# Loads reordered, and the folded matrix M built during batch 0's exps, in an attention and maxout MoE kernel

## The chip, the cores and the metric

The kernel runs on one core of one Trainium2 chip. The metric is device microseconds of one execution, as the median of the runs. The engines are TensorE (PE in the profile; PEld is its weight load), VectorE (DVE), ScalarE (ACT), GpSimd (POOL) and SyncE (SP). Each has an instruction queue of its own, which it works through in program order. Loads that convert float32 to bfloat16 on the way are issued by GpSimd; plain loads of q and k by SP.

## What is computed

Blockwise causal attention feeds a maxout MoE layer. Batch 8, heads 8, sequence 576, head size 64; d_model 512, d_ff 1024, 4608 tokens.

```python
scores = scale * np.matmul(q, k.transpose(0, 1, 3, 2))
mask = block_i >= block_j            # blocks of 64 positions
attn = softmax(np.where(mask, scores, -1e9))
x = np.matmul(attn, v).transpose(0, 2, 1, 3).reshape(B * S, H * D)
h1 = x @ w1
h2 = x @ w2
g = np.maximum(h1, h2)
out = g @ w_out
```

## The kernel before, in words

**Work units.** Two heads make a pair, four pairs a batch, two pairs a group (GPB is 2 groups per batch, NG 16 groups). Batch 0 (groups 0 and 1) is written out by hand in lines 578 to 682; groups 2 to 15 follow, group 2 partly in the hand-written part, groups 3 to 15 in the loop at line 684.

**Attention.** load_qk (L112) loads q and k of a group as float32, with SP or ACT as issuer; with gated=True GpSimd first writes one element of the new buffer (L119), so that the load is issued only when GpSimd has come to that point of its program. cast (L126) makes bfloat16, for the groups after the first two on GpSimd (L132). transposes (L346) turns q or k on TensorE (18 matmuls, L352) and copies the result out with two engines (L360), mostly half on VectorE and half on ScalarE. A burst (L402) or a tile (L432 to L457) puts scores of 512 columns in one of two PSUM buffers ps_s (L371), and one ScalarE exp (L395) writes them to aT; mask (L399) clears masked parts by memset. av (L463) multiplies by V (L479), and VectorE divides by the row sums (L485 and L486) into xp. x_out (L503) transposes xp on TensorE (L517, L519) and copies it into xT (L522, L523); from group 4 on a DMA transposes it instead. pad_keys (L377) copies the corner keys kz on GpSimd (L378). load_v (L134) loads one chunk of 128 rows of V through GpSimd (L136).

**MoE.** max(xw1, xw2) is computed as max(x(w1 - w2), 0) + xw2. d_sb = w1 - w2 comes from diff_w on VectorE (L162), in four quarters of 256 columns. The part xw2 is folded into the output: M = w2 w_out, so that out = max(xd, 0) w_out + xM. bT_unit (L223) transposes a quarter of w2 (8 matmuls, L227) into bT_sb (L229); m_unit (L234) makes one eighth of M (8 matmuls of 256 columns, L238). h_unit (L202) makes one of 8 column blocks of xd for a span of tokens (L215) and VectorE clips it to g (L220). y_unit (L252) sums 4 + 8 matmuls into 128 rows of the output (L257), which VectorE (first two spans) or ScalarE copies (L262) and SP stores. Spans 0 and 1 are the first 256 and the next 320 tokens, that is batch 0; later spans have 512 tokens. All MoE units, x_out, av and the transposes take their PSUM tiles from one pool of four buffers (tag "m"). warm_up (L338) runs matmuls on zeros that nothing reads (L341).

**Buffers for w2.** w2 has no tile of its own: it lies in parts of xT that later batches fill (L146 to L150).

**What sets the order.** plan (L285) writes a list of units with the tokens each needs and its cost per matmul (1 for 512 columns). fill(n) (L322) issues matmuls until n of cost are spent, each time from the first unit of the list whose tokens are there. In the list before, span 0's h units are mixed with the bT units, and the M units come behind span 1's h units. fill_of (L534) sets how much a group gets: the ready work less 6, spread over the groups left until the next batch. In groups 3 to 15 two ninths of it, at least 3, go ahead of each pair's av, an eighteenth, at least 3, into the middle of each av, and the rest to the end of the group. The loads are issued in program order of GpSimd's queue: V chunks 0 and 1, a quarter each of w1 and w2, V chunks 2 to 4, then the other quarters, and then the two halves of w_out (L168). Group 2's q is loaded by SP at the start, its k after V chunk 4.

Of the kernel before, what the change touches and what calls it, by code (L numbers as in the profile page):

```python
# [14 lines left out]
def kernel(  # L15
# [96 lines left out]
    def load_qk(g, queues, gated=False):  # L112
        b, u = divmod(g, GPB)
        for nm, src, queue in (("q", q, queues[0]), ("k", k, queues[1])):
            if queue is None:
                continue
            raws[nm, g] = t = raw.tile([P, 2, RPP * D], FP32, name=f"{nm}raw")
            if gated:
                nc.gpsimd.memset(t[:, 0, :1], 0.0)  # L119
            queue.dma_start(  # L120
                out=t[:],
                in_=src[b, 4 * u:4 * u + 4].rearrange(
                    "(s h) (p t) d -> (h p) s (t d)", h=2, t=RPP),
            )

    def cast(nm, g, parts):  # L126
        t = raws[nm, g].rearrange("p s (t d) -> p t s d", d=D)
        if (nm, g) not in qk_n:
            qk_n[nm, g] = qkn.tile([P, RPP, 2, D], BF16, name=f"{nm}n")
        n = qk_n[nm, g]  # L130
        for copy, j0, j1 in parts:
            copy(out=n[:, j0:j1], in_=t[:, j0:j1])  # L132
# [10 lines left out]
    wor = moe_w_out.rearrange("(c p) f -> p c f", p=P)  # L143

    WB = 256
    w1_raw, w2_sb = {}, []  # L146
    for j in range(d_ff // WB):
        row, n = (1, j) if j < 3 else (3, 0)
        t0 = 3 * S - 3 * BLK + n * NDM * WB
        w2_sb.append(xT[:, row, t0:t0 + NDM * WB].rearrange("p (c f) -> p c f", c=NDM))  # L150

    def load_w(j, which=(0, 1)):
        fs = slice(j * WB, (j + 1) * WB)
        if 0 in which:
            w1_raw[j] = wraw.tile([P, NDM, WB], FP32, name="w1raw")
            nc.gpsimd.dma_start(out=w1_raw[j][:], in_=w1r[:, :, fs])
        if 1 in which:
            nc.gpsimd.dma_start(out=w2_sb[j], in_=w2r[:, :, fs])

    def diff_w(j):  # L160
        fs = slice(j * WB, (j + 1) * WB)
        nc.vector.tensor_sub(d_sb[:, :, fs], w1_raw[j][:], w2_sb[j])  # L162

    WH = d_model // 2

    def load_wo(i):
        ds = slice(i * WH, (i + 1) * WH)
        nc.gpsimd.dma_start(out=wo_sb[:, :, ds], in_=wor[:, :, ds])  # L168
# [8 lines left out]
    nc.vector.memset(zeros[:], 0.0)  # L177
    nc.scalar.activation(out=warm[:], in_=warm[:], func=AF.Exp)
    load_qk(1, (SP, SP))
    load_qk(2, (SP, None))  # L180
    make_identity(nc, ident)
    for r in range(NV):
        nc.vector.memset(vv_r[r][:, :, :, D:D + 1], 1.0)
# [6 lines left out]
    cast("k", 0, ((act, 0, 5), (dve, 5, RPP)))  # L190
    for c in range(2):
        load_v(0, c)
    load_w(0, (0,))
    cast("q", 1, ((pool, 7, RPP),))
    cast("k", 1, ((pool, 0, 7),))
    load_w(0, (1,))


    done_tokens = [0]
# [23 lines left out]
    def bT_unit(j):  # L223
        pt = ps_m.tile([P, 2, NDM, P], BF16, name="ps_bT", tag="m")
        for i in range(2):
            for c in range(NDM):
                nc.tensor.transpose(pt[:, i, c, :], w2_sb[j][:, c, i * P:(i + 1) * P], ident[:])  # L227
                if i == 1 and c == NDM - 1:
                    nc.vector.tensor_copy(  # L229
                        out=bT_sb[:, 2 * j:2 * j + 2, :],  # L230
                        in_=pt.rearrange("p i c d -> p i (c d)"))
                yield

    def m_unit(i, c):  # L234
        ds = slice(i * WH, (i + 1) * WH)
        pt = ps_m.tile([P, WH], FP32, name="ps_M", tag="m")
        for f in range(NFF):
            nc.tensor.matmul(  # L238
                pt[:], bT_sb[:, f, c * P:(c + 1) * P], wo_sb[:, f, ds],
                start=(f == 0), stop=(f == NFF - 1),  # L240
            )
            if f == NFF - 1:
                nc.vector.tensor_copy(out=m_sb[:, c, ds], in_=pt[:])
            yield
# [40 lines left out]
    def plan():  # L285
        def h(i, f):
            t0, w = spans[i]
            units.append((h_unit(i, f), t0 + w, w / SPAN, NDM))

        def y(i, s, last=False):  # L290
            t0, w = spans[i]
            if last:
                units.append((y_last(i, s), t0 + w, 0.333, 3 * NY))
            else:
                units.append((y_unit(i, s), t0 + w, 1.0, NY))

        for i in range(NSPAN):
            for f in range(NFF):
                h(i, f)
                if i == 0 and f % 2:  # L300
                    units.append((bT_unit(f // 2), 0, 0.25, 2 * NDM))
                if i > 2 and f % 2 == 0 and f // 2 < tiles[i - 1]:
                    y(i - 1, f // 2)
            if i == 1:
                for n in range(2 * NDM):
                    units.append((m_unit(n // NDM, n % NDM), 0, 0.5, NFF))
                for j in range(2):
                    for s in range(tiles[j]):
                        y(j, s)
        n = tiles[-1]  # L310
        for s in range(n):
            y(NSPAN - 1, s, s == n - 1)
# [25 lines left out]
    def warm_up(n):  # L338
        pw = ps_m.tile([P, SPAN], FP32, name="ps_w", tag="m")
        for _ in range(n):  # L340
            nc.tensor.matmul(pw[:], zeros[:, :P], zeros[:], start=True, stop=True)  # L341
# [4 lines left out]
    def transposes(nm, g, copies):  # L346
        n = qk_n.pop((nm, g))
        pts = [ps_m.tile([P, RPP, NP], BF16, name=f"ps_{nm}T", tag="m") for _ in range(2)]
        for j in range(RPP):
            for i in range(2):  # L350
                r = slice(i * NP, (i + 1) * NP)
                nc.tensor.transpose(  # L352
                    pts[i][:, j, :], n[r, j].rearrange("p s d -> p (s d)"), ident[r, r],
                )

        def copy_out(which=(0, 1), part=(0, NP), copy=None):
            p0, p1 = part
            for i in which:
                t = (qT_r if nm == "q" else kT_r)[(2 * g + i) % NT]
                (copy or copies[i])(  # L360
                    out=t[:, p0 * RPP:p1 * RPP].rearrange("q (p j) -> q p j", j=RPP),
                    in_=pts[i][:, :, p0:p1].rearrange("q j p -> q p j"),
                )
        return copy_out
# [12 lines left out]
    def pad_keys(p):  # L377
        nc.gpsimd.tensor_copy(  # L378
            out=kz_r[p % NT].rearrange("p (a c) -> p a c", c=BLK)[:, 0:3:2],
            in_=kT_r[p % NT][:, S - 3 * BLK:].rearrange("p (a c) -> p a c", c=BLK)[:, 0:3:2],  # L380
        )
# [31 lines left out]
    def burst_q1(p):  # L413
        burst(p, ((0, QCUT, 320), (1, QCUT, 192)), 384)

    def burst_q2(p):
        burst(p, ((1, 448, P), (2, QCUT, 320), (4, 512, BLK)), 896)
# [4 lines left out]
    def masks_p(p, eng=None):  # L422
        for a in (0, 256):
            mask(p, a, eng)

    def masks_q(p, eng=None):
        for a in (1024, 1408):
            mask(p, a, eng)
# [3 lines left out]
    def tile_0(p):  # L432
        u = ps_s.tile([P, 2, 512], FP32, name="ps_s", tag="s")
        scores(p, u, 0, 0, 0, 512)
        return lambda: (exp(p, u, 512, 0), mask(p, 0))

    def tile_1(p):
        u = ps_s.tile([P, 2, 512], FP32, name="ps_s", tag="s")
        scores(p, u, 0, 0, 512, 64)
        scores(p, u, 64, 1, 128, 448)  # L440
        return lambda: (exp(p, u, 512, 512), mask(p, 576))
# [147 lines left out]
    burst_p(1)  # L589
    warm_up(2)  # L590
    masks_p(1)
    for c in range(2, NCH):
        load_v(0, c)
    load_qk(2, (None, SP), gated=True)
    load_w(1)
    cq = transposes("q", 1, (dve, dve))
    burst_q1(0)
    ck = transposes("k", 1, (dve, dve))
# [15 lines left out]
    masks_p(3, nc.vector)  # L614
    burst_q2(0)
    av(2, [0, 1])
    warm_up(2)
    x_out(0, 0, 2, (act, act))
    av(3, [0, 1])
    diff_w(0)  # L620
    burst_q1(1)
    warm_up(2)
    cast("q", 2, ((pool, 0, RPP),))
    masks_q(0)
    load_w(2)
    burst_q2(1)
    x_out(1, 0, 2)
    warm_up(2)
    burst_q3(1)
    masks_q(1)  # L630
    load_w(3)
    fill(4)
    burst_q1(2)
    transposes("q", 2, (dve, act))()
    burst_q2(2)
    av(0, [2, 3, 4])
    burst_q3(2)
    masks_q(2)
    cast("k", 2, ((pool, 0, RPP),))
    load_wo(0)  # L640
    load_wo(1)
    av(1, [2, 3, 4])
    burst_q1(3)
    burst_q2(3)
    av(2, [2, 3, 4])
    transposes("k", 2, (dve, act))()
    burst_q3(3)
    masks_q(3)
    pad_keys(4)
    pad_keys(5)  # L650
    for c in range(NCH):
        load_v(1, c)
    load_qk(3, (SP, SP), gated=True)
    x_out(0, 2, NCH)
    fill(2)
    diff_w(1)
    outs = tile_0(4), tile_1(4)
    av(3, [2, 3, 4])
    region(*outs)
    x_out(1, 2, NCH)  # L660
    fill(4)
    diff_w(2)
    fill(2)
    region(tile_2(4), tile_0(5))
    fill(4)
    diff_w(3)
    fill(2)
    region(tile_1(5), tile_2(5))
    fill(4)
    fill(2)  # L670
    cast("q", 3, ((pool, 0, RPP),))
    cast("k", 3, ((pool, 0, RPP),))
    n = fill_of(GPB)
# [86 lines left out]
```

## Time and profile before

| what | value |
|---|---|
| time, median of 3 runs (lowest, highest) | 260.99 us (260.83, 261.69) |
| the profiled execution: its time, its span | 260.99 us, 259.2 us |
| busy share of the span, PE / PEld / DVE / ACT / POOL | 94% / 54% / 53% / 55% / 42% |
| chain that ended last, share of the span | PE 85%, DMA 5%, POOL 3%, issue 2%, ACT 2% |
| weight and V loads by GpSimd's queue: packets, MB | 42272, 8.92 |
| q and k loads and stores by SP's queue: packets, MB | 28544, 31.27 |

The span runs from the first to the last instruction; the time also holds what lies around it, 1.8 us here. A row of a timeline gives the start, the length, the engine, the line of the kernel, the operation, out<-in and the number of instructions; in square brackets it gives the engine's idle time ahead of it and what ended that. A matmul's listed length holds its way through the array, so a matmul that follows another costs less than its length: the difference of two starts is its price. The times of loads below run from the issue to the landing of the last byte.

### The profile page before, as it was taken

The numbers are of one execution on the slowest core, as the hardware profiler recorded it, in microseconds if no ns is written. First come the engines' busy times: TensorE is split into PE (matmuls) and PEld (weight loads), VectorE is DVE, ScalarE is ACT, GpSimd is POOL, SyncE is SP. The second block draws the span as 40 slices with busy tenths as digits, with TensorE's granted clock in tenths as the row PEclk, the third lists the DMA queues.
The fourth block names the chain that finished last, engine by engine and source line by source line (L and its number), as shares of the span: only waits on it lengthen the run. The fifth ranks groups of instructions, "written<-read, shape, count | busy, mean of one in ns | idle before, by whom it ended". The sixth has DMA issues, their size and how long they took to land.

```text
span 259.2 us, 7161 instructions
## 1 busy us (share of the span) xinstructions
PE 244.8 (94%) x2949; PEld 139.4 (54%) x2983; DVE 137.6 (53%) x301; ACT 141.3 (55%) x198; POOL 109.8 (42%) x274
## 2 busy tenths in 40 slices
PE   8688799999999999999999999999999999999995
PEld 3346566856555545454646464646464655444444
DVE  4967996646584518451855185518550853453200
ACT  2798552766665766576657665776577431100111
POOL 2987914475638163816381638263823010000000
DMA  7999998789579995998599949984986122202122
GB/s 245 317 204 310 194 241 146 280 73 275 111 184 250 135 195 136 238 149 215 129 236 139 179 163 239 141 208 139 90 106 116 44 51 83 83 0 81 43 104 99
DMA packets 71265, 41.30 MB, mean 159 GB/s; under 512 B 53568, under 2 KB 58048, under 8 KB 71232
## 3 DMA queue, kind: packets, MB, share of 16 engines
q1 hardware_dynamic: 28544, 31.27, 41.4%
q0 software_dynamic: 42272, 8.92, 38.2%
q10 hardware_dynamic: 416, 0.66, 0.7%
q8 instruction: 23, 0.38, 0.6%
q14 instruction: 10, 0.08, 0.1%
HBM read 34.60 MB, written 9.44 MB: 170 GB/s over the span
## 4 chain that ended last, share of the span: by engine, by line
PE 85%; DMA 5%; POOL 3%; issue 2%; ACT 2%; DVE 1%; POOLq 0%; ACTq 0%
PE ps_y L257 35%; PE ps_h L215 22%; PE ps_o L479 10%; PE ps_s L371 8%; DMA qraw<-in_q_dram 5%; PE ps_M L238 3%; PE ps_qT L352 2%; PE ps_kT L352 2%; POOL vv L136 1%; ACT aT L395 1%; PE ps_y L272 1%; DVE qn L132 1%; PE ps_w L341 1%; PE ps_s L389 1%; POOL wo_sb L168 1%
## 5 line engine op out<-in xcount | busy, mean ns | idle before, releaser
L395 ACT ACTIVATE aT<-ps_s 128x1024 bf16<-128x1024 f32 (+2 forms) x100 | 95.9, 996 | 28.6 <-PE ps_s L371 26.6
L215 PE MATMUL ps_h<-xT,d_sb 128*128 128x512 bf16 (+3 forms) x306 | 67.4, 357 | 2.7 <-DVE d_sb L162 1.2
L257 PE MATMUL ps_y<-wo_sb,g 128*128 128x512 bf16 x275 | 69.1, 379 | 0.4 <-issue 0.3
L220 DVE TENSOR_SCALAR g<-ps_h 128x512 bf16<-128x512 f32 (+3 forms) x80 | 50.8, 636 | 30.2 <-PE ps_h L215 28.4
L400 POOL MEMSET aT<- 64x128 bf16 x124 | 22.4, 199 | 85.1 <-ACT aT L395 84.4
L485 DVE RECIPROCAL rec<-ps_o 128x4 f32<-128x4 f32 (+1 forms) x64 | 12.0, 188 | 62.7 <-PE ps_o L479 61.9
L215 PEld LDWEIGHTS <-d_sb 128*128 128x128 bf16 x320 | 29.1, 98 | 30.1 <-issue 2.7
L479 PEld LDWEIGHTS <-aT 128*128 128x128 bf16 x960 | 37.2, 98 | 13.5 <-issue 0.8
L262 ACT COPY y<-ps_y 128x512 f32<-128x512 f32 x31 | 18.2, 587 | 44.8 <-PE ps_y L257 32.6
L257 PEld LDWEIGHTS <-g 128*128 128x128 bf16 x280 | 25.9, 98 | 29.7 <-issue 1.9
L479 PE MATMUL ps_o<-vv,aT 128*128 128x65 bf16 x960 | 39.8, 194 | 0.0
L257 PE MATMUL ps_y<-m_sb,xT 128*128 128x512 bf16 x128 | 36.5, 380 | 1.2 <-issue 0.8
L136 POOL DMA_DIRECT2D vv<-in_v_dram x40 | 33.6, 847 | 1.6 <-issue 1.2
L371 PE MATMUL ps_s<-qT,kT 64*128 64x64 bf16 (+6 forms) x344 | 31.0, 280 | 1.9 <-ACT kT L360 0.7
L486 DVE TENSOR_TENSOR xp<-ps_o,rec 128x256 bf16<-128x256 f32 (+1 forms) x64 | 31.4, 491 | 2.2
L360 ACT COPY qT<-ps_qT 128x576 bf16<-128x576 bf16 (+1 forms) x17 | 10.3, 614 | 20.0 <-PE ps_qT L352 20.0
L132 POOL CAST qn<-qraw 128x1152 bf16<-128x1152 f32 (+1 forms) x16 | 17.0, 1061 | 8.7 <-DMA qraw<-in_q_dram 8.7
L257 PEld LDWEIGHTS <-xT 128*128 128x128 bf16 x140 | 12.2, 98 | 15.1 <-issue 3.5
L371 PEld LDWEIGHTS <-kT 64*128 64x128 bf16 x344 | 12.2, 94 | 11.0 <-issue 6.2
L132 POOL CAST kn<-kraw 128x1152 bf16<-128x1152 f32 (+1 forms) x15 | 17.1, 1141 | 1.4 <-DMA kraw<-in_k_dram 1.3
L360 ACT COPY kT<-ps_kT 128x576 bf16<-128x576 bf16 x15 | 9.6, 639 | 14.6 <-PE ps_kT L352 14.6
L207 POOL COPY g<-g 128x512 bf16<-128x512 bf16 x8 | 4.9, 613 | 20.7 <-DVE g L220 20.3
(57 smaller groups left out, 160.8 us busy)
## 6 DMA issues: line engine op xcount, KB each, us to landing
qraw<-in_q_dram SPq DMA_DIRECT2D x16, 576.0 KB, 4.1
out_dram<-y SPq DMA_DIRECT2D x35, 256.0 KB, 3.2
kraw<-in_k_dram SPq DMA_DIRECT2D x15, 576.0 KB, 5.4
vv<-in_v_dram POOLq DMA_DIRECT2D x32, 128.0 KB, 5.2
w1raw<-in_moe_w_dram POOLq DMA_DIRECT2D x4, 512.0 KB, 8.7
xT<-in_moe_w_dram POOLq DMA_DIRECT2D x4, 256.0 KB, 9.1
wo_sb<-in_moe_w_out_dram POOLq DMA_DIRECT2D x2, 512.0 KB, 9.0
kraw<-in_k_dram ACTq DMA_DIRECT2D x1, 576.0 KB, 5.5
```

Source lines behind the costliest of these rows:

```text
L132: copy(out=n[:, j0:j1], in_=t[:, j0:j1])
L136: nc.gpsimd.dma_start(out=vv_r[b % NV][P - rows:, c, :, :D], in_=v[b, :, c * P:c * P + rows, :].rearrange("h p d -> p h d"),)
L215: nc.tensor.matmul(pt[:, :w], d_sb[:, c, f * P:(f + 1) * P], xT[:, c, t0:t0 + w], start=(c == 0), stop=(c == NDM - 1),)
L220: nc.vector.tensor_scalar_max(g[:, f, m:m + w], pt[:, :w], 0.0)
L257: nc.tensor.matmul(py[:], lhs, rhs, start=(n == 0), stop=(n == len(terms) - 1),)
L262: (dve if i < 2 else act)(out=y[:], in_=py[:])
L360: (copy or copies[i])(out=t[:, p0 * RPP:p1 * RPP].rearrange("q (p j) -> q p j", j=RPP), in_=pts[i][:, :, p0:p1].rearrange("q j p -> q p j"),)
L371: nc.tensor.matmul(ps[:, hh, col:col + w], kT[r, k0:k0 + P], qT[r, q0:q0 + w], start=True, stop=True,)
L395: nc.scalar.activation(out=aT_r[p % NA][:, :, a0:a0 + w], in_=ps[:, :, :w], func=AF.Exp, scale=scale,)
L400: (eng or nc.gpsimd).memset(aT_r[p % NA][BLK:, :, a0:a0 + BLK], 0.0)
L479: nc.tensor.matmul(po[:, gi, hh, :], a[:, hh, a0:a0 + P], vv[:, c, h0 + 2 * hh, :], start=(mm == 0), stop=(mm == n_mm - 1),)
L486: nc.vector.tensor_mul(xp[:, :, ts[0]:ts[0] + n, p % 2].rearrange("q s t d -> q t s d"), po[:, :, :, :D], rec[:, :n].to_broadcast([P, n, 2 ...
```

## The change

- w2 is loaded in two halves of 512 columns rather than four quarters, ahead of everything but V chunks 0 and 1; the halves lie in two rows of xT.
- Half of w_out comes next, then V chunks 2 to 4, the other half of w_out, and then the four quarters of w1.
- Group 2's q and k are both loaded behind a gate after pair 1's masks; the q load at the start and the k load after V chunk 4 go away. Their casts and transposes move behind the last exp of batch 0.
- In the plan's list all bT units come first, then all M units, then span 0's h units.
- In the hand-written part three warm_up(2) become fill(2), further fills stand between the exps of pairs 2 and 3 and later, and av, x_out, diff_w and the transposes of group 2 are placed anew.

The functions fill, fill_of and ready are the same in both.

```diff
--- before.py
+++ after.py
@@ -143,23 +143,23 @@
     wor = moe_w_out.rearrange("(c p) f -> p c f", p=P)
 
     WB = 256
-    w1_raw, w2_sb = {}, []
-    for j in range(d_ff // WB):
-        row, n = (1, j) if j < 3 else (3, 0)
-        t0 = 3 * S - 3 * BLK + n * NDM * WB
-        w2_sb.append(xT[:, row, t0:t0 + NDM * WB].rearrange("p (c f) -> p c f", c=NDM))
-
-    def load_w(j, which=(0, 1)):
-        fs = slice(j * WB, (j + 1) * WB)
-        if 0 in which:
-            w1_raw[j] = wraw.tile([P, NDM, WB], FP32, name="w1raw")
-            nc.gpsimd.dma_start(out=w1_raw[j][:], in_=w1r[:, :, fs])
-        if 1 in which:
-            nc.gpsimd.dma_start(out=w2_sb[j], in_=w2r[:, :, fs])
+    w1_raw = {}
+    WC = d_ff // 2
+    w2_sb = [
+        xT[:, row, 3 * S - 3 * BLK:3 * S - 3 * BLK + NDM * WC].rearrange("p (c f) -> p c f", c=NDM)
+        for row in (1, 3)]
+
+    def load_w1(j):
+        w1_raw[j] = wraw.tile([P, NDM, WB], FP32, name="w1raw")
+        nc.gpsimd.dma_start(out=w1_raw[j][:], in_=w1r[:, :, j * WB:(j + 1) * WB])
+
+    def load_w2(i):
+        nc.gpsimd.dma_start(out=w2_sb[i], in_=w2r[:, :, i * WC:(i + 1) * WC])
 
     def diff_w(j):
-        fs = slice(j * WB, (j + 1) * WB)
-        nc.vector.tensor_sub(d_sb[:, :, fs], w1_raw[j][:], w2_sb[j])
+        n = j * WB % WC
+        nc.vector.tensor_sub(
+            d_sb[:, :, j * WB:(j + 1) * WB], w1_raw[j][:], w2_sb[j * WB // WC][:, :, n:n + WB])
 
     WH = d_model // 2
 
@@ -177,7 +177,6 @@
     nc.vector.memset(zeros[:], 0.0)
     nc.scalar.activation(out=warm[:], in_=warm[:], func=AF.Exp)
     load_qk(1, (SP, SP))
-    load_qk(2, (SP, None))
     make_identity(nc, ident)
     for r in range(NV):
         nc.vector.memset(vv_r[r][:, :, :, D:D + 1], 1.0)
@@ -190,10 +189,10 @@
     cast("k", 0, ((act, 0, 5), (dve, 5, RPP)))
     for c in range(2):
         load_v(0, c)
-    load_w(0, (0,))
+    load_w2(0)
     cast("q", 1, ((pool, 7, RPP),))
     cast("k", 1, ((pool, 0, 7),))
-    load_w(0, (1,))
+    load_w2(1)
 
 
     done_tokens = [0]
@@ -223,8 +222,9 @@
     def bT_unit(j):
         pt = ps_m.tile([P, 2, NDM, P], BF16, name="ps_bT", tag="m")
         for i in range(2):
+            f = 2 * j + i
             for c in range(NDM):
-                nc.tensor.transpose(pt[:, i, c, :], w2_sb[j][:, c, i * P:(i + 1) * P], ident[:])
+                nc.tensor.transpose(pt[:, i, c, :], w2_sb[f // (NFF // 2)][:, c, f % (NFF // 2) * P:(f % (NFF // 2) + 1) * P], ident[:])
                 if i == 1 and c == NDM - 1:
                     nc.vector.tensor_copy(
                         out=bT_sb[:, 2 * j:2 * j + 2, :],
@@ -294,16 +294,16 @@
             else:
                 units.append((y_unit(i, s), t0 + w, 1.0, NY))
 
+        for n in range(NFF // 2):
+            units.append((bT_unit(n), 0, 0.25, 2 * NDM))
+        for n in range(2 * NDM):
+            units.append((m_unit(n // NDM, n % NDM), 0, 0.5, NFF))
         for i in range(NSPAN):
             for f in range(NFF):
                 h(i, f)
-                if i == 0 and f % 2:
-                    units.append((bT_unit(f // 2), 0, 0.25, 2 * NDM))
                 if i > 2 and f % 2 == 0 and f // 2 < tiles[i - 1]:
                     y(i - 1, f // 2)
             if i == 1:
-                for n in range(2 * NDM):
-                    units.append((m_unit(n // NDM, n % NDM), 0, 0.5, NFF))
                 for j in range(2):
                     for s in range(tiles[j]):
                         y(j, s)
@@ -589,10 +589,12 @@
     burst_p(1)
     warm_up(2)
     masks_p(1)
+    load_wo(0)
     for c in range(2, NCH):
         load_v(0, c)
-    load_qk(2, (None, SP), gated=True)
-    load_w(1)
+    load_wo(1)
+    for j in range(d_ff // WB):
+        load_w1(j)
     cq = transposes("q", 1, (dve, dve))
     burst_q1(0)
     ck = transposes("k", 1, (dve, dve))
@@ -614,60 +616,61 @@
     masks_p(3, nc.vector)
     burst_q2(0)
     av(2, [0, 1])
-    warm_up(2)
+    fill(2)
     x_out(0, 0, 2, (act, act))
     av(3, [0, 1])
-    diff_w(0)
     burst_q1(1)
-    warm_up(2)
-    cast("q", 2, ((pool, 0, RPP),))
+    fill(2)
     masks_q(0)
-    load_w(2)
     burst_q2(1)
     x_out(1, 0, 2)
-    warm_up(2)
+    fill(2)
     burst_q3(1)
     masks_q(1)
-    load_w(3)
-    fill(4)
+    load_qk(2, (SP, SP), gated=True)
+    fill(2)
     burst_q1(2)
-    transposes("q", 2, (dve, act))()
     burst_q2(2)
-    av(0, [2, 3, 4])
+    fill(4)
+    fill(4)
     burst_q3(2)
     masks_q(2)
-    cast("k", 2, ((pool, 0, RPP),))
-    load_wo(0)
-    load_wo(1)
-    av(1, [2, 3, 4])
     burst_q1(3)
+    fill(4)
+    fill(4)
     burst_q2(3)
-    av(2, [2, 3, 4])
-    transposes("k", 2, (dve, act))()
+    av(0, [2, 3, 4])
     burst_q3(3)
     masks_q(3)
+    cast("q", 2, ((pool, 0, RPP),))
+    cast("k", 2, ((pool, 0, RPP),))
+    av(1, [2, 3, 4])
+    x_out(0, 2, NCH)
+    av(2, [2, 3, 4])
+    diff_w(0)
+    fill(4)
+    transposes("q", 2, (dve, act))()
+    av(3, [2, 3, 4])
+    fill(4)
+    transposes("k", 2, (dve, act))()
     pad_keys(4)
     pad_keys(5)
     for c in range(NCH):
         load_v(1, c)
     load_qk(3, (SP, SP), gated=True)
-    x_out(0, 2, NCH)
-    fill(2)
     diff_w(1)
-    outs = tile_0(4), tile_1(4)
-    av(3, [2, 3, 4])
-    region(*outs)
     x_out(1, 2, NCH)
     fill(4)
+    region(tile_0(4), tile_1(4))
+    fill(4)
     diff_w(2)
-    fill(2)
+    fill(4)
     region(tile_2(4), tile_0(5))
     fill(4)
     diff_w(3)
-    fill(2)
+    fill(4)
     region(tile_1(5), tile_2(5))
     fill(4)
-    fill(2)
     cast("q", 3, ((pool, 0, RPP),))
     cast("k", 3, ((pool, 0, RPP),))
     n = fill_of(GPB)
```

More of the change, by code (lines that the diff above doesn't have):

```diff
@@ L616 @@
     av(2, [0, 1])
-    warm_up(2)
+    fill(2)
     x_out(0, 0, 2, (act, act))
     av(3, [0, 1])
-    diff_w(0)
     burst_q1(1)
-    warm_up(2)
-    cast("q", 2, ((pool, 0, RPP),))
+    fill(2)
     masks_q(0)
-    load_w(2)
     burst_q2(1)
     x_out(1, 0, 2)
-    warm_up(2)
+    fill(2)
     burst_q3(1)
     masks_q(1)
-    load_w(3)
+    load_qk(2, (SP, SP), gated=True)
+    fill(2)
+    burst_q1(2)
+    burst_q2(2)
     fill(4)
-    burst_q1(2)
-    transposes("q", 2, (dve, act))()
-    burst_q2(2)
-    av(0, [2, 3, 4])
+    fill(4)
     burst_q3(2)
     masks_q(2)
-    cast("k", 2, ((pool, 0, RPP),))
-    load_wo(0)
-    load_wo(1)
-    av(1, [2, 3, 4])
     burst_q1(3)
+    fill(4)
+    fill(4)
     burst_q2(3)
-    av(2, [2, 3, 4])
-    transposes("k", 2, (dve, act))()
+    av(0, [2, 3, 4])
     burst_q3(3)
     masks_q(3)
+    cast("q", 2, ((pool, 0, RPP),))
[9 more added lines that the diff above has]
+    transposes("k", 2, (dve, act))()
     pad_keys(4)
```

## The prediction

> **What bounds the kernel now.** I read the stages first (each engine's busy time by stretch), then TensorE's waits, then the timeline of the stretch that is left. The stages from the start, with length, busy time of PE, PEld, DVE, ACT and POOL, granted clock, DMA share and GB/s:
>
> ```profile
> 0.00:15.00 15.00, 10.77 (x127) 4.96 (x130) 10.48 (x32) 8.14 (x13) 9.74 (x23) 1.00 1.11 270
> 15.00:41.00 26.00, 21.93 (x366) 15.55 (x367) 21.05 (x48) 16.79 (x24) 16.35 (x35) 1.00 1.48 234
> 41.00:90.00 49.00, 48.15 (x718) 30.56 (x724) 30.48 (x68) 30.46 (x42) 26.52 (x67) 1.00 0.88 181
> 90.00:240.00 150.00, 147.89 (x1644) 79.69 (x1665) 73.45 (x152) 82.38 (x115) 57.19 (x150) 1.00 0.72 138
> ```
>
> From 41 us on TensorE is idle for 0.85 of 49 and 2.1 of 150 us: it is the bound, and its work there is a fixed sum. Only two things can move the end: idle time of PE before steady work, and the warm-up matmuls, which compute nothing. Up to 15 us the diff touches no PE instruction. From 15 to 41 us 26.00 - 21.93 = 4.07 us are idle. PE's waits between 14 and 42 us (total, times, longest) say what for:
>
> ```profile
> PE ps_xe L517 <- DVE xp L486: 1.2, 1, 1.2
> PE ps_h L215 <- DVE d_sb L162: 1.2, 2, 0.6
> PE ps_s L371 <- ACT aT L395: 0.7, 2, 0.4
> PE ps_qT L352 <- POOL qn L132: 0.6, 1, 0.6
> ```
>
> The first two are VectorE's: it runs late by its four weight subtractions (L162, 1.22 us each). The last is the end of a chain that runs through GpSimd, which issues the loads. Its timeline (start, length, idle before):
>
> ```profile
> 26.55 0.53 POOL L378 COPY kz<-kT 128x128 bf16<-128x128 bf16 x2
> 27.02 4.18 POOL L136 DMA_DIRECT2D vv<-in_v_dram  x5
> 31.16 0.15 POOL L119 MEMSET qraw<- 128x1 f32 x1
> ...
> 39.03 1.14 POOL L132 CAST qn<-qraw 128x1152 bf16<-128x1152 f32 x1 [2.89 <-DMA qraw<-in_q_dram]
> ```
>
> Group 2's k transposes (24.47) free the kz copies, then five V issues, then the memset that gates the load of group 3's q: issued by SP at 31.34, landed 7.6 us later. PE gets it at 40.23.
>
> **What the change removes and adds.** All sums are against the profiled execution: 260.99 us with a span of 259.2; the median of the runs is the same 260.99.
>
> *Warm-ups.* Three warm_up(2) go: six 512-column matmuls at about 0.215 us start to start (the listed 0.38 each includes the drain) = 1.3 us less of PE. In their places stand bT transposes, 8 in 0.54 us each, which replace work done later. By the rows this costs no clock: the granted clock is 1.00 in every stretch, across PE's 1.17 us idle before 12.03 too. The Trainium skill (TensorE: Matmul & The Clock Gate, Part 1) speaks against removing warm-ups, since an idle window of some 3.4 us halves the clock; by it, one such window costs up to 1.7 us, but no idle stretch here or in my walk below is half as long.
>
> *M in batch 0's exps.* 32 bT transposes (2.2 us) and 64 M matmuls (12 in 1.42 us, 0.118 each: 7.55 us) move ahead of h. The sum of PE's work is unchanged. Fills before the group-2 planner come to 56 units of cost in place of 24; so the planner, with 124 units of batch-0 work in all, gives groups 2, 3, 4 fills of 21, 21, 20 in place of 32, 31, 31, and both leave 6. From group 5 on the schedules agree, so whatever PE has saved by then is saved at the end.
>
> *Loads.* Before, the GpSimd queue's transfers land in order: w1 and w2 quarters 14.2 to 29.9, w_out 32.5 and 35.1. After: two V chunks as now (12), w2's halves, w_out half 0, late V, w_out half 1, then w1. No row shows a w2 half: bounds are one quarter's spacing, 1.2 us (landings 26.1 to 27.2), and a w_out half's, 2.6 (32.5 to 35.1); I take two quarters, 2.4, and with the issue of half 1 at 10.2 get landings of 14 and 16.2. Then w_out half 0 at 18.8, three V chunks (3.7 us before, part of it waiting for the issue) 21 to 22.5, half 1 at 23.6 to 25.1, and w1 at 1.4 a quarter (27.2 to 28.6), from 25 to 26.5. q2 and k2 cut in: with k2 in flight one w1 quarter took 2.65 (19.8 to 22.45), 1.25 more, so two cost 2.5; at the 406 GB/s of 4 to 6 us they cost 2.9. First w1 quarter 27.5 to 29.4, taken as 28.4; last 32.6. GpSimd issues are cheap: two w2 issues fewer save 2 x 0.75, and the rest (0.88, 3 x 0.82, 0.88, 4 x 0.77) end at 18.9, just ahead of the exps that the next masks wait for (19.3 now).
>
> *q2 and k2 move late*, from the start and 14.15 to about 19.8 on SP, with one gate memset more (0.11). Nothing else is queued on SP until 31. Landing 7.6 to 8.4 us later as at 14.15 and 31.34: 27.5 to 28.5. Their casts (1.18, 1.15) run on GpSimd after the last mask, 28 to 30.5; PE asks at 29.2 and 31.5. That is covered, by under a microsecond.
>
> *A walk of PE from 15 us*, with the rows' durations. bT(0) to bT(3) stand at the warm-ups' places; each drain takes VectorE 0.69, in place of the 1.22 subtraction at 17.23; bT(1) waits 0.2 for a PSUM buffer. M units from 19.8 (w_out landed at 18.8); batch 0's last exp ends at 26.1 (26.0 before, so ScalarE loses nothing). x_out(0,2) stands right behind av(1): its reciprocal and multiply take 0.2 + 0.56 with two hand-overs, so PE idles 0.9. Then diff_w(0), 29.0 to 30.2 on VectorE, with M's drain and half the q copy queued behind it: PE loses 0.4 for a buffer, 0.7 at x_out(1,2), 0.4 at the M unit behind it. Together 2.6; with 0.3 for small hand-overs (before shows four of 0.2) 2.9. The two stalls for d_sb go, since M work lies between the subtractions and h.
>
> *Group 3's chain again.* k2 transposed at 31.5; its copy by VectorE done at 33.3; kz 0.5, V issues 4.2, gate, SP: q3 is issued at 38.2. Landing 4.1 to 4.6 as at 56.2 and 67.7, where V also runs (at 31.34 w_out was still ahead), and the cast 1.15: q3 ready at 43.5 to 44.0. PE asks at 43.9. q4 follows 7.1 after q3 (40.2 and 47.24 in before), but PE now asks for it 6.3 us on, not 8.1, as the fills between are 7 units shorter: 50.2 against 50.6 to 51.1. I take a stall of 0.7.
>
> *Groups 3 and 4* shrink from 11 to about 8.3 us of PE. ScalarE needs 7.75 (six exps 0.97 to 1.03, two of 0.27, two copies 0.64), and the first tile of the next group waits for the second PSUM buffer: 0.2 to 0.3 each, 0.5 in all.
>
> **Sum.** Loss before: 4.07 + 1.3 = 5.4. Loss after: 2.9 + 0.7 + 0.5, and 0.2 for a w1 a little late: 4.3. Gain 1.1: **259.9 us**, own range 259.0 to 260.6 (each of the three terms off by its half, added).
>
> **Rivals.**
> *The third group's chain sets the end (slower).* Its place is the q3 load at 38.2, behind V. For it: 31.34, where V was also in flight, took 7.6. Against: 56.2 and 67.7. At 7.6 q3 is ready at 47.0, q4 at 54.1, the stall 3.9 in place of 0.7: 263.1. It decides from a landing of 5.5, where the stall is 1.8 and the gain gone. The rows show neither equal shares nor order of arrival: the DMA queues show no packet of SP's queue from 31.4 to 35, though q3 was issued at 31.34. The Trainium skill (DMA: Bandwidth & Descriptors, Queues, rings and completion order) says that an engine serves its queues in turn, packet by packet. By it, as an estimate, q3 beside V runs at half rate, 1.5 us more than alone, lands in 5.2 and gives 260.6; nothing above uses this.
> *The weights come late, VectorE blocks.* With w2's halves at 2.6, V at 3.7 and q2 and k2 at 2.9, w1's first quarter lands at 30 to 31, not by 29.0; VectorE waits with the M drain and q copy behind it, and PE follows after its four buffers. 1 to 2 us lost: 260.9 to 261.9. For it: the DMA share of 1.48 in this stretch, the highest of all. Against: the bytes ahead of w1 are those of before less q2 and k2.
> *The cover is better than I walk it.* VectorE catches up, q3 lands in 3.7 as at 42.3, w2 in 1.2: the stalls shrink to 1.7 and 0.2: 258.5.
> *It does not do what it says.* The drawing function is the same text in both, and if w_out's half lands after 20, M stands still in the exps: the gain shrinks to the warm-ups less the new stalls, within 0.3 of before. I count it with the late weights.
>
> **Chances.** Forecast 0.38, better cover 0.12, late weights (or an idle change) 0.22, chain 0.28. The measurement tells about 0.3%, 0.8 us, from no change. Faster by more: 0.34 of the forecast and the 0.12 = 0.46. Within: 0.04 of the forecast, 0.10 of late weights, 0.02 of the chain = 0.16. Slower: 0.12 + 0.26 = 0.38. The range for 8 in 10 reaches from the better cover to the chain's 263.1: 258.4 to 263.2.
>
> **What would show it.** PE's idle between 15 and the q3 transposes near 2.9 us, with the longest wait 0.9 before L517 and none for d_sb; M matmuls between 20 and 35; L162 at 29 and not waiting for a DMA; the q3 transposes at 43.5 to 45; the wait of the q4 transposes for qn under 1 us. Wrong if PE waits over 1.5 us for qn or for wo_sb, if VectorE waits for w1raw, or if groups 3 and 4 leave PE idle over 1 us.

## The result and the profile after

The changed kernel takes 270.36 us (median of 4 runs, 269.73 to 271.51) against 261.19 for the kernel before on the same chip; the ratio is 1.0355, 95% interval 1.0315 to 1.0394. The forecast was 259.9. The profiled execution took 270.37 us with a span of 268.6, 9.4 more than that of before.

One row dates the loss. On SyncE's queue the first DMA transpose (group 4's) is a mark that both kernels pass with the same work done. In the timeline of before, and then of the changed kernel:

```profile
76.53 1.30 SPq L497 DMA_TRANSPOSE xT<-xp  x1
```

```profile
85.94 1.30 SPq L497 DMA_TRANSPOSE xT<-xp  x1
```

From the mark to the end it is 182.7 and 182.7 us. So all 9.4 us are lost ahead of it. The stages of the changed kernel in that stretch (start:end, length, busy time of PE, PEld, DVE, ACT and POOL, granted clock as a share of full speed, DMA share, GB/s):

```profile
15.00:30.00 15.00, 13.23 (x224) 10.05 (x223) 9.36 (x28) 9.04 (x13) 5.41 (x15) 1.00 1.51 256
30.00:33.00 3.00, 0.00 (x0) 0.00 (x0) 1.04 (x2) 0.00 (x0) 1.11 (x1) 0.97 0.94 328
33.00:36.50 3.50, 3.42 (x50) 2.82 (x50) 1.51 (x3) 0.64 (x1) 1.17 (x2) 0.53 0.10 35
36.50:47.60 11.10, 10.56 (x122) 7.35 (x120) 10.01 (x20) 7.10 (x9) 7.06 (x17) 1.00 1.04 88
47.60:52.00 4.40, 0.16 (x7) 0.11 (x7) 0.53 (x2) 0.00 (x0) 1.14 (x1) 0.76 0.54 187
52.00:55.50 3.50, 3.50 (x30) 2.05 (x28) 1.74 (x3) 0.64 (x1) 1.23 (x3) 0.50 0.27 61
55.50:60.00 4.50, 4.35 (x49) 2.30 (x49) 2.28 (x5) 2.53 (x3) 2.68 (x6) 0.86 0.74 247
```

TensorE stands still for 3.5 us (from 29.6) and for 4.2 (from 47.7), and behind each stop it works at half clock: until about 36.3 us behind the first, until about 56.7 behind the second. TensorE's waits, 14 to 90 us (total, times, longest):

```profile
PE ps_qT L352 <- POOL qn L132: 7.7, 2, 4.2
PE ps_s L371 <- ACT aT L451: 0.9, 2, 0.5
PE ps_xe L517 <- DVE xp L486: 0.9, 1, 0.9
...
PE ps_M L238 <- DMA wo_sb<-in_moe_w_out_dram: 0.5, 1, 0.5
```

The two stops are for q of group 2 and q of group 3 (q2 and q3 below; k2 is k of group 2). The account: 7.7 us of waiting; at lowered clock 3.5 x 0.47 + 3.5 x 0.50 + 4.5 x 0.14 = 4.0 us of TensorE's work; together 11.7. Since only 9.4 are lost, the rest of the change gained 2.3. GpSimd's timeline says why q came late:

```profile
14.88 0.92 POOL L168 DMA_DIRECT2D wo_sb<-in_moe_w_out_dram  x1
15.74 1.57 POOL L154 DMA_DIRECT2D w1raw<-in_moe_w_dram  x2
17.94 0.76 POOL L154 DMA_DIRECT2D w1raw<-in_moe_w_dram  x1 [0.63 <-DMA xT<-in_moe_w_dram]
20.56 0.75 POOL L154 DMA_DIRECT2D w1raw<-in_moe_w_dram  x1 [1.87 <-DMA wo_sb<-in_moe_w_out_dram]
...
22.02 0.10 POOL L119 MEMSET qraw<- 128x1 f32 x1
...
31.89 1.14 POOL L132 CAST qn<-qraw 128x1152 bf16<-128x1152 f32 x1 [5.24 <-DMA qraw<-in_q_dram]
35.10 1.15 POOL L132 CAST kn<-kraw 128x1152 bf16<-128x1152 f32 x1 [2.07 <-DMA kraw<-in_k_dram]
37.87 1.45 POOL L378 COPY kz<-kT 128x128 bf16<-128x128 bf16 x2 [1.63 <-DVE kT L360]
39.27 4.21 POOL L136 DMA_DIRECT2D vv<-in_v_dram  x5
43.43 0.17 POOL L119 MEMSET qraw<- 128x1 f32 x1
...
50.70 1.14 POOL L132 CAST qn<-qraw 128x1152 bf16<-128x1152 f32 x1 [4.31 <-DMA qraw<-in_q_dram]
```

GpSimd itself waited at the third and the fourth w1 load, so the gate of q2 and k2 passed at 22.0. SP issued them at 22.15 and 22.56; they landed 9.6 and 12.4 us later. With k2 all that follows is late: kz, the V issues, the gate of q3 at 43.4, and then 7.0 us of landing. What ran beside q2 and k2 is in the DMA queues (packets, MB, share of 16 engines), first from 22.2 to 26 us, then from 26 to 31:

```profile
q0 software_dynamic: 939, 1.07, 131.7%
q1 hardware_dynamic: 10, 0.02, 1.8%
```

```profile
q0 software_dynamic: 312, 1.14, 63.8%
q1 hardware_dynamic: 310, 0.68, 40.5%
```

q0 is GpSimd's queue, q1 SP's. Until 26 us next to nothing of q2 and k2 moved, while late V and w_out's second half, issued ahead of them, did (w_out landed at 25.8). From then on w1's queue and SP's moved as many packets each; but w1's packets are larger, so q2 and k2 got 37% of the bytes (0.68 of 1.82). The Trainium skill (DMA: Bandwidth & Descriptors, Queues, rings and completion order) states a taking of turns by packet; the second pair of rows agrees with it, the first does not (10 packets of 949), and neither does the stretch behind q3's issue, where from 43.6 to 45 us GpSimd's queue moved 1517 packets of V and SP's none. My prediction had quoted the rule for q3 and not used it. Why SP's packets came so late the traces do not say.

### The profile page after: what moved, and what is told of

Its sections match the earlier page's. It is cut to its first block, busy times and chain, and to the rows that moved or that the text cites. A ratio compares the mean times of both kernels' runs of the same rounds, so it can differ in the third digit from the quotient of the medians.

```text
span 268.6 us, 7139 instructions
## 1 busy us (share of the span) xinstructions
PE 247.5 (92%) x2943; PEld 140.3 (52%) x2977; DVE 137.5 (51%) x301; ACT 141.6 (53%) x198; POOL 109.1 (41%) x273
## 3 DMA queue, kind: packets, MB, share of 16 engines
q1 hardware_dynamic: 28544, 31.27, 39.5%
## 4 chain that ended last, share of the span: by engine, by line
PE 78%; DMA 12%; POOL 4%; ACT 2%; issue 2%; DVE 0%; SPq 0%; POOLq 0%; ACTq 0%
PE ps_y L257 33%; PE ps_h L214 22%; PE ps_o L479 10%; PE ps_s L371 6%; DMA qraw<-in_q_dram 6%; DMA wo_sb<-in_moe_w_out_dram 3%; DMA kraw<-in_k_dram 3%; PE ps_qT L352 2%; PE ps_kT L352 2%; ACT aT L395 1%; POOL vv L136 1%; PE ps_y L272 1%; POOL qn L132 1%; PE ps_s L389 1%; PE ps_M L238 1%
## 5 line engine op out<-in xcount | busy, mean ns | idle before, releaser
L214 PE MATMUL ps_h<-xT,d_sb 128*128 128x512 bf16 (+3 forms) x307 | 68.9, 365 | 1.4 <-issue 1.0
L400 POOL MEMSET aT<- 64x128 bf16 x124 | 22.2, 200 | 83.7 <-ACT aT L395 83.1
L479 PEld LDWEIGHTS <-aT 128*128 128x128 bf16 x960 | 37.8, 98 | 14.3 <-issue 0.5
L214 PEld LDWEIGHTS <-d_sb 128*128 128x128 bf16 x320 | 29.8, 100 | 29.4 <-issue 3.0
L479 PE MATMUL ps_o<-vv,aT 128*128 128x65 bf16 x960 | 40.4, 195 | 0.1
L360 DVE COPY qT<-ps_qT 128x576 bf16<-128x576 bf16 (+1 forms) x17 | 12.1, 711 | 7.2 <-PE ps_qT L352 7.1
```

The costliest lines, as they stand in the source:

```text
L214: nc.tensor.matmul(pt[:, :w], d_sb[:, c, f * P:(f + 1) * P], xT[:, c, t0:t0 + w], start=(c == 0), stop=(c == NDM - 1),)
L360: (copy or copies[i])(out=t[:, p0 * RPP:p1 * RPP].rearrange("q (p j) -> q p j", j=RPP), in_=pts[i][:, :, p0:p1].rearrange("q j p -> q p j"),)
L400: (eng or nc.gpsimd).memset(aT_r[p % NA][BLK:, :, a0:a0 + BLK], 0.0)
L479: nc.tensor.matmul(po[:, gi, hh, :], a[:, hh, a0:a0 + P], vv[:, c, h0 + 2 * hh, :], start=(mm == 0), stop=(mm == n_mm - 1),)
```

## The experiments

The theory after this: q2 and k2 are issued late and land late, q3 hangs on them, each wait counts once, and a long wait halves the clock. The rival of the whole series: the DMA engines are full in this stretch, and whatever is moved ahead is paid by what it is moved ahead of.

**x1_qk_before_w1**

```diff
     load_wo(1)
+    load_qk(2, (SP, SP), gated=True)
     for j in range(d_ff // WB):
         load_w1(j)
...
-    load_qk(2, (SP, SP), gated=True)
     fill(2)
```

> The changed kernel with one line moved: group 2's q and k are gated right behind w_out's second half, ahead of the four w1 loads, in place of behind pair 1's masks. Theory (the loads behind a gate are late, and each microsecond that TensorE waits for q2 or q3 counts once, plus 1.7 us for a half clock behind each wait over about 3 us): the gate passes at 15.8 in place of 22.0, the q2 wait of 3.46 us and its half clock go, and q3 is asked for at 44 and is there at 46.4 (issue 38.2, landing 7.0 as in the changed kernel), a wait of 2.4 without a half clock: 270.4 - 3.5 - 1.7 - 1.8 - 1.7 = 261.7 us. Rival (the DMA engines are the bound and all of w2, w_out, V, w1, q2 and k2 has to land anyway): what q2 gains, w_out's second half and w1 lose, TensorE waits for them instead, 268 us or more.

Measured 270.78 us (267.35 to 273.77), ratio 1.033 (1.026 to 1.040): no gain in the median. The q2 wait is gone, and the whole wait is now at q3 (TensorE's waits, 14 to 90 us):

```profile
PE ps_qT L352 <- POOL qn L132: 5.3, 1, 5.3
...
PE ps_M L238 <- DMA wo_sb<-in_moe_w_out_dram: 0.9, 1, 0.9
PE ps_o L479 <- DMA vv<-in_v_dram: 0.5, 2, 0.3
```

I had expected 2.4 us at q3. Its gate passed at 40.3, not 38, and the load took 7.7 us. In the profiled execution the mark is passed at 82.9, 3.0 earlier than in the changed kernel: 3.5 + 1.65 us were won at q2, and of that 1.1 went to q3 and 0.9 to w_out and V. The two waits stand in series: a part of what is won at the first is waited for at the second. The others of the four executions had a lower mean clock (0.975 to 0.981, against 0.992) and took 3 to 6 us more. As an estimate, the share of clock missing times the span, less the same for the profiled execution, gives up to 3.0 of the 3.1 and 3.8 us of two of them, and up to 4.7 of the 6.4 of the third; why the clock was lower there no trace shows.

**x2_q3_before_v**

```diff
+    load_qk(3, (SP, SP), gated=True)
     for c in range(NCH):
         load_v(1, c)
-    load_qk(3, (SP, SP), gated=True)
```

> The changed kernel with group 3's q and k gated ahead of batch 1's five V loads in place of behind them. Theory: the gate passes at 39.3 in place of 43.4, q3 lands in 3.7 to 4.6 us without V ahead of it, is cast by 45.2 and TensorE asks at 47.6: that wait (4.24 us) and the half clock behind it (1.7) go, the q2 wait stays: 264.4 us. Rival (q3 is slow because the engines are full, not because V is ahead): a wait of 2 us or more stays, 268 us.

Measured 265.72 us (264.15 to 267.28), ratio 1.0185 (1.013 to 1.024), 1.3 above the theory and 2.3 below the rival. q3 was issued at 40.5 and landed in 3.9 us; TensorE no longer waits for it. q2's wait of 3.3 us stays, and behind it the clock is half until about 39.3 us (0.57 from 35 to 40), some 2.6 us of work in place of the 1.7 of the theory, which is 0.9 of the 1.3. So most of the 7.0 us for q3 in the changed kernel came from V ahead of it, not from full engines.

**x3_both** (the two diffs above together)

> Both moves together. Theory: no wait over 1 us for q2 or q3 and the granted clock 1.00 throughout: 270.4 - 3.46 - 4.24 - 2 x 1.7 = 259.3 us. Rival (full DMA engines): 266 us or more, with the waits at w_out, V or d_sb.

Measured 263.02 us (262.44 to 267.66), ratio 1.007 (1.005 to 1.009). Neither q2 nor q3 is waited for, but the time is 3.7 over the expectation. The stages of the profiled execution (262.44 us) say what is left in it:

```profile
20.00:25.00 5.00, 3.93 (x41) 3.08 (x38) 1.57 (x4) 3.28 (x4) 1.73 (x7) 1.00 1.43 291
25.00:30.00 5.00, 3.55 (x77) 2.69 (x75) 2.17 (x6) 1.51 (x2) 1.94 (x4) 0.95 1.28 305
30.00:35.00 5.00, 5.00 (x80) 3.87 (x77) 3.95 (x9) 0.64 (x1) 0.69 (x1) 0.71 0.62 210
```

TensorE is idle for 2.5 of the 10 us from 20 on, in stops of at most 1.1 (w_out, V, VectorE's division), and the clock falls all the same: 5 x 0.29 + 5 x 0.05 = 1.7 us of work. q2 and k2, now ahead, made w_out's first half land at 21.2, not 20.3, and TensorE wait 0.6 for the late V: the rival's price, though a small one. The clock is not the whole of it: another execution had a mean clock of 1.000 and took 263.00 us all the same, and no trace shows where.

**x4_dummies**

```diff
+    warm_up(15)
     transposes("q", 2, (dve, act))()
...
+    warm_up(19)
     transposes("q", 3, (dve, act))()
```

> The changed kernel with matmuls on zeros in the two waits: 15 ahead of group 2's q transposes, 19 ahead of group 3's, about 3.2 and 4.1 us, a little less than the waits. Nothing else moves. Theory (the idle time itself halves the clock, which costs 1.7 us behind each wait): the granted clock is 1.00 throughout and the time 270.4 - 3.4 = 267.0 us. Rival (the slow matmuls behind the waits come from something else, such as memory traffic): no gain, 270 us.

Measured 268.34 us (267.45 to 268.77), ratio 1.028 (1.025 to 1.030), with the granted clock at 0.998 to 1.000 in all four executions. So the idle time itself halved the clock. The gain is 2.0 us, not 3.4. In the profiled execution the gate of q2 passed 1.05 us later than in the changed kernel (23.07 against 22.02), which by itself moves the chain, and the zeros ahead of q3 outlasted the wait: q3 was cast at 51.4, its transposes started at 52.2.

**x5_two_w1**

```diff
-    for j in range(d_ff // WB):
+    for j in range(2):
         load_w1(j)
...
-        w1_raw[j] = wraw.tile([P, NDM, WB], FP32, name="w1raw")
+        t = wraw.tile([P, NDM, WC], FP32, name="w1raw")
```

> The changed kernel with w1 loaded in two halves in place of four quarters, so that GpSimd issues eleven weight and V loads ahead of the gate, not thirteen; the gates stay where they are. In the changed kernel the twelfth and the thirteenth waited 0.63 and 1.87 us on GpSimd for the landing of the fourth and the fifth. Theory (a load on this queue waits for the eighth before it to land, and that held up the gate): GpSimd shows no wait at a load's issue, q2 is issued at 19.8 in place of 22.15, q2 and k2 land some 2.3 us earlier, and as the chain through k2, kz, V and q3 sets the end, the time is 270.4 - 2.3 = 268 us, with a q2 wait of about 1 us and a q3 wait of 4 to 6. Rival (q2 and k2 are late because the engines are full until 34, whenever they are issued): they land at the same time as before and the time stays at 270 us.

Measured 268.71 us (266.98 to 269.90), ratio 1.027 (1.024 to 1.030): 1.7 us won. GpSimd shows no wait at a load's issue; q2 is issued at 20.6 and lands at 30.3 (31.75 in the changed kernel), k2 at 34.3 (35.0). Both theories hold in part: the issue is 1.5 us earlier, the landings only 1.4 and 0.7, and q2 and k2 still take 9.7 and 13.3 us; from 25 to 30 us w1 again has two thirds of the bytes (1.27 of 1.98 MB). TensorE waits 2.6 us for q2 and 5.1 for q3 in the profiled execution, and behind the 2.6 the clock stays at 1.00.

**x6_undo_qk**

```diff
     load_qk(1, (SP, SP))
+    load_qk(2, (SP, None))
...
         load_v(0, c)
+    load_qk(2, (None, SP), gated=True)
     load_wo(1)
...
-    load_qk(2, (SP, SP), gated=True)
```

> The changed kernel with one part of the change undone: group 2's q is loaded by SP at the start and its k behind a gate after the late V, as in the kernel before; its casts and transposes stay where the change put them, as do all weight loads and the MoE order. Theory (the late load of q2 and k2 is the larger part of the loss, the rest hangs on q3's chain): no q2 wait and no half clock behind it; w2 and w_out come 1 to 1.5 us later, since q2 again goes ahead of them, so TensorE waits about 2 us for w_out at the first M unit; q3 stays late by 2 to 4 us: 265.5 us. Rival (M in batch 0's exps and the order of the weights cost the time, not q2 and k2): 269 us or more.

Measured 270.65 us (268.87 to 271.83), ratio 1.036 (1.033 to 1.039): nothing won, 5 over the expectation and in the range of the rival. The part of the change that I held to be the culprit can't be undone alone. TensorE's timeline at the first M units, and behind the scores the next two (this kernel has one line more, so L239 is L238 above):

```profile
23.87 3.59 PE L239 MATMUL ps_M<-wo_sb,bT_sb 128*128 128x256 bf16 x16 [2.65 <-DMA wo_sb<-in_moe_w_out_dram]
27.40 0.77 PE L372 MATMUL ps_s<-qT,kT 64*128 64x192 bf16 x6
28.10 2.73 PE L239 MATMUL ps_M<-wo_sb,bT_sb 128*128 128x256 bf16 x16
```

w_out's first half lands at 23.8, 3.5 us later; TensorE waits 2.65, then runs 16 M matmuls in 3.59 us that took 1.92, and later it waits 5.0 for q3 all the same. M in batch 0's exps needs w2 and w_out by 20 us: with q2 and k2 ahead of them w_out is late, with q2 and k2 behind them these are.

**x7_best**: both gates moved (x3_both), and

```diff
     burst_q2(2)
+    warm_up(4)
     fill(4)
...
-    x_out(0, 2, NCH)
     av(2, [2, 3, 4])
+    x_out(0, 2, NCH)
...
-    diff_w(1)
     x_out(1, 2, NCH)
     fill(4)
+    diff_w(1)
```

> Both moves of the gates (x3_both) and three more: av(2) goes ahead of x_out(0, 2, NCH), so that the 0.9 us for VectorE's division is covered; diff_w(1) goes behind x_out(1, 2, NCH) and the fill after it; four matmuls on zeros stand ahead of the first M unit, where TensorE waits 0.5 to 1.1 us for w_out, to keep the clock. Theory (the rest of the loss of x3_both is half clock and these short waits): 263.0 - 0.9 - 1.4 = 260.7 us or a little less, the granted clock 1.00. Rival (the loads of w2 and w_out set a floor for this order): 262 us or more, with longer waits at w_out or V.

Measured 260.92 us (259.90 to 263.27, 12 executions), ratio 0.9998 (0.998 to 1.002): the time of the kernel before, 9.4 us less than the changed kernel, and near the 260.7 of the theory. The granted clock is 0.998 to 1.000 in eleven of twelve executions. What is left is the wait for w_out, 1.3 us behind the four matmuls on zeros.

**x8_gate_mid_w1**: x7_best with the gate of q2 and k2 behind the second w1 load, and warm_up(2).

> x7_best with group 2's q and k gated between the second and the third w1 load, in place of ahead of the first, and two matmuls on zeros ahead of the first M unit in place of four. In x7_best q2 and k2 landed at 23.2 and 25.5 while TensorE asks for them at 30.6 and 32.8, and they cut in on w_out's first half, which landed at 22.0, not 20.3. Theory (w_out's first half sets when M can start, and any load moved ahead of it is paid there): w_out lands at 20.3 again, the wait of 1.3 us plus two of the four zeros go, q2 is still in time: 260.9 - 1.6 = 259.3 us. Rival (q2 and k2 beside w1's large packets are late again): TensorE waits over 1 us for q2 and the time stays at 261 or above.

Measured 261.25 us (260.63 to 262.89), ratio 1.001 (0.999 to 1.003): missed by 2. The waits only changed hands (TensorE's, 14 to 60 us, and one of VectorE's):

```profile
PE ps_M L238 <- DMA wo_sb<-in_moe_w_out_dram: 1.0, 2, 0.6
PE ps_o L479 <- DMA vv<-in_v_dram: 0.9, 2, 0.6
```

```profile
DVE d_sb L161 <- DMA w1raw<-in_moe_w_dram: 1.2, 1, 1.2
```

The time is the rival's, but not its mechanism: TensorE does not wait for q2. It is the rival of the whole series that fits: w_out's first half landed at 20.9, not 20.3, its second half at 30.2 (25.8 in the changed kernel), and TensorE or VectorE waits for these, the late V and w1 in its place.

**x9_no_zeros**: x7_best without warm_up(4).

> x7_best without the four matmuls on zeros ahead of the first M unit; TensorE then stands still there for about 2.1 us in place of 1.3. Theory (the clock is halved not only by one long wait but by a stretch with much idle time, such as 20 to 30 us here, and zeros hold it): the time is the same where the clock holds, and 1.5 us or more longer where it does not; granted clock under 0.998 in about half of the executions, median 261.8 us. Rival (only a single wait of over 3 us halves the clock): 1.00 throughout and 260.9 us, as x7_best.

Measured 261.84 us (259.91 to 264.26, 12 executions), ratio 1.002 (0.999 to 1.005). Six executions have a granted clock of 0.999 to 1.000 and a median of 260.6 us; the other six 0.987 to 0.993 and 262.9. The profiled execution is one of the second six (two stages, and TensorE's first M units):

```profile
20.00:25.00 5.00, 2.44 (x19) 1.60 (x14) 0.70 (x2) 1.94 (x2) 1.53 (x6) 0.78 1.44 290
25.00:30.00 5.00, 5.00 (x64) 3.48 (x62) 1.59 (x5) 2.39 (x3) 0.20 (x1) 0.88 1.32 288
```

```profile
22.80 3.58 PE L238 MATMUL ps_M<-wo_sb,bT_sb 128*128 128x256 bf16 x16 [2.56 <-DMA wo_sb<-in_moe_w_out_dram]
```

A stop of 2.56 us was enough to halve the clock here, and in other executions the same program kept it. With the four matmuls on zeros, 0.86 us, one execution in twelve lost clock (x7), without them six. The two runs were made on different chips and with twelve executions each, so the effect of the zeros is likely, not proved; the rival, no loss of clock without a wait of over 3 us, is refuted.

**x10_before_q3_first**: the kernel before with the gate of q3 ahead of batch 1's V, as in x2_q3_before_v.

> The kernel before the change with one line moved: group 3's q and k gated ahead of batch 1's five V loads in place of behind them. Theory (the gate behind V is worth as much as TensorE waits for q3, and no more): q3 lands before TensorE asks at 40, the wait of 0.62 us goes, and what follows it in the chain (q4) is earlier too: 261.0 - 0.6 = 260.4 us. Rival (the V loads then land too late for batch 1's av, or q3 is slow behind w_out anyway): no change, 261.0 us, with the wait still there or moved to V.

Measured 260.70 us (260.28 to 261.63, 12 executions) against 261.13, ratio 0.9986 (0.9975 to 0.9998): a little faster than both kernels. q3 is cast at 36.2, not 39.0, and TensorE's wait of 0.6 for it is gone. The rival is right in one thing: with w_out still ahead of it q3 took 7.4 us to land; what helped is the issue at 27.1, not 31.3. The gate and the V issues:

```profile
26.95 0.11 POOL L119 MEMSET qraw<- 128x1 f32 x1
26.99 0.12 POOL L119 MEMSET kraw<- 128x1 f32 x1
27.03 4.18 POOL L136 DMA_DIRECT2D vv<-in_v_dram  x5
36.15 1.14 POOL L132 CAST qn<-qraw 128x1152 bf16<-128x1152 f32 x1
```

## Why the prediction was wrong, point by point

- **The bound and the frame: right.** TensorE's fixed work sets the end, the schedules agree from group 5 on (182.6 to 182.7 us from the mark to the end in all kernels here but x5, with 183.0), and the end moves by what is lost ahead of it.
- **The walk without the chain: near in sum, by some luck.** I forecast a loss of 3.6 us apart from the q waits (2.9 + 0.5 + 0.2) in place of 5.4, a gain of 1.8; the account above gives 2.3. x_out's 0.9 and the vanished d_sb waits are as forecast; groups 3 and 4 cost 0.9, not 0.5; w_out 0.5, not nothing. But of the 1.5 us for VectorE's backlog behind diff_w(0) (0.4, 0.7 and 0.4) TensorE's waits show at most 0.3 (at an M unit): errors of both signs cancelled.
- **"q2 and k2 move late ... That is covered, by under a microsecond": the step that failed first.** I had SP's issue at 19.8 and landings of 27.5 to 28.5. Measured: 22.15, with landings at 31.8 and 35.0. Three things were missing. GpSimd held its own loads back (2.5 us in all; without that, in x5, the issue comes 1.5 us earlier and the landings 1.4 and 0.7). SP's load then moved almost nothing for 3.8 us, until what GpSimd had issued ahead was through. And from 26 us q2 and k2 shared the engines with w1, whose packets are larger. I took the rows of 14.15 and 31.34, which by the trace are 8.0 and 7.6 us; 8.4 was the median of q and k at 31.34, and k's own 9.1 I left out. In those rows SP's queue waited as well (27 packets of 2758 from 14.2 to 17), but then got most of the bytes (0.50 of 0.79 MB from 17 to 20, 1.14 of 1.32 from 35 to 39.5). The rows to look for were the DMA queues with their packet counts and sizes.
- **"Landing 4.1 to 4.6 as at 56.2 and 67.7": the second.** It was 7.0. At 56.2 two V loads were nearly done, here all five had been issued just ahead. The row of 31.34 was the nearer one, and I set it aside since w_out was still ahead there. x2 shows 3.9 us as soon as the gate stands ahead of V (3.9 to 4.0 in x3 and x7); x10, with w_out still ahead, 7.4, so w_out there was a reason too.
- **"no idle stretch here or in my walk below is half as long": the third.** I set the rule of the Trainium skill (TensorE: Matmul & The Clock Gate, Part 1) aside because the walk had no long stop. A rule on stops has to be laid against the rivals too: with the chain late, the half clock added 4.0 us. The page's window of some 3.4 us agrees with the stretches at half clock here, 3.4 us (32.9 to 36.3) and 6.8 (49.9 to 56.7), twice as long. Its threshold does not: x3 and x9 show the clock falling after shorter stops, and in x5 it held after one of 2.6 us.
- **The rivals.** The chain was named, with a chance of 0.28, but only from q3 on and without the clock, so its 263.1 was 7 us short. Its first link, k2, I had costed as covered. Nor do all sums of the prediction come out: half of 2.9, 0.7 and 0.5 adds up to 2.05, wider than the own range of 259.0 to 260.6, and the better cover gives 258.2 by its terms, not 258.5; neither bears on the miss. Late w1 was not what decided (VectorE does not wait for w1 in the changed kernel); it appears in x8.
- **What stays open.** Why three of four executions of x1 were slower than the profiled one; where x3 loses its time in the execution with full clock; why SP's load waits until GpSimd's earlier loads are through; and whether an order exists in which neither q2 nor w_out is waited for: x7 and x8 suggest that it would need fewer bytes ahead of 30 us, which was not tried.

## What to carry to other kernels

A load that is moved behind a gate is priced by the gating engine's whole queue, its own waits for earlier loads among them, and by what is under way ahead of it and beside it in the DMA queues (here almost nothing moved for 3.8 us, then 37% of the bytes); and then the chain of gates behind it is walked to the end before it is called covered. Put the small load that an engine will ask for first ahead of the bulk that is asked for later: for q3 that one line was worth 4.6 us in the changed kernel and 0.4 in the one before. A forecast of a few microseconds on a TensorE-bound kernel should price a stop of 2.5 us and more at its length and, with a chance, 1.6 to 2.6 us of half clock on top (1.6 and 2.4 in the changed kernel, 2.6 in x2, none behind q2 in x5 and none in half of x9's executions).

## What the runs showed of the hardware that I had not expected

- In these programs a load on GpSimd's queue waited for the landing of the eighth load ahead of it: the twelfth waited for the fourth (0.63 us) and the thirteenth for the fifth (1.87), in the changed kernel, and likewise in x2, x3 and x4; with eleven loads (x5) there was no wait. Whether that is the chip's or the program's semaphores the traces do not say.
- The clock can fall without a long stop (x3: stops of at most 1.1 us, a quarter of 10 us idle, then 0.71 from 30 to 35 us), and not in every execution.
- GpSimd's two kz copies took 1.45 us in the changed kernel and 0.53 in the one before. Beside the 1.45 VectorE ran diff_w(1), a subtraction with two inputs (37.72 to 38.93); in x7, with diff_w(1) moved behind, they took 0.53. The Trainium skill (SBUF — State Buffer, SBUF: two separate sides) says that a VectorE instruction with two SBUF inputs contends with a GpSimd instruction that reads SBUF, through a port that they share, and these rows fit that.
- w2 in halves showed no gain: the halves landed 2.6 us apart (15.0 and 17.6), against the 2.4 that I had taken for two quarters.
